# Adding the three shifted bit patterns of an exponential quad on GpSimd as 64-bit integers instead of on VectorE as 16-bit values

## The chip, the core and the metric

The kernel runs on one core of a Trainium2 chip. The metric is the device time of one execution in microseconds (us), taken as the median of several runs. A core has five engines with a queue of instructions each, which they work off in order and which wait for each other by semaphores: TensorE (PE in the profile, with its weight loads as PEld), ScalarE (ACT), VectorE (DVE), GpSimd (POOL) and SyncE (SP, which here issues the transfers).

## The reference

Two branches over the same input `x` (2048 x 512) are mixed by a gate: softmax attention with 32 heads of width 16, and a long convolution whose filter is a sum of complex exponentials.

```python
def _A_ref(x, wqkv, wo):                       # attention, H = 32, Dh = 16
    qkv = (x @ wqkv).reshape(B, S, 3, H, Dh) ...
    scores = jnp.einsum("bhqd,bhkd->bhqk", q, k) * Dh ** -0.5
    p = _softmax(scores, axis=-1)
    return jnp.einsum("bhqk,bhkd->bhqd", p, v) ... @ wo
def _B_ref(u, ...):                            # K = Re sum C dB exp(logdA * l); y = conv(u, K) + u * Dskip
    ...
g = _sigmoid((x * gate_w).sum(-1, keepdims=True))
return g * _A_ref(...) + (1 - g) * _B_ref(...)
```

The change lies in the exponential of the softmax. 32 heads x 2048 queries x 2048 keys are 134 million exponentials.

## The kernel before

**Tiles.** The scores are made in tiles of 128 keys x 512 queries of one head, 2048 tiles in all. Three tiles form a group; there are 683 groups, numbered `g`. A group's scores are written by `qk(g)` into one of two PSUM tensors of three banks, `SC[g % 2]`. `ex(g)` is one ScalarE activation (line 961 in the profile) over the group: it reads the scores from PSUM and writes bf16 exponentials to the ring `ET` (or `EX`, which is more of the same ring). `pv(q)` multiplies the exponentials of four heads (a quad) with the values and sums them in the PSUM bank `OA`; a column of ones among the values gives the softmax's denominator.

**Exponentials on VectorE.** For some quads the exponential is not made by ScalarE. In four groups that follow each other, the third tile of the group goes to VectorE instead, so that ScalarE's activation of such a group covers two tiles (128x1024) and not three (128x1536). VectorE's `bits(g)` (line 982) reads that tile from PSUM, multiplies and adds, and writes the result as a 16-bit integer into a quarter of the tile `DZ`: read as bf16 this bit pattern is a coarse power of two. When four quarters are there, `batch(i)` (line 996) makes three copies `DU` of all 2048 columns, each with another constant of `CUTS = (26, 56, 94)` added to the 16-bit pattern. `sums(i)` multiplies `DZ` and the three `DU` with the values, so that each such exponential is a sum of four coarse ones. Four tiles, their three adds and four products make a set `i`. Which groups give a tile is settled in `decide`, by the two windows in

```python
WIN = ((110,560,2,5,0,1),(560,678,4,5,0,2))
```

(first and last group, number of `DZ` tiles, least distance of two sets in groups, a budget that is 0 here, number of `DU` triples). A set is taken when its distance is kept, when no more than one set per 5.3 groups would have been taken, and by a planner's estimate of how far VectorE and ScalarE are: `idle()` is the later of the two engines' planned ends less VectorE's planned busy time, and `slow` in `win` widens the least distance to 9 groups while the convolution's filter blocks (`K0` to `K15`, built with VectorE) are behind a due line.

**Order.** All orders are planned in Python while the kernel is built. `Prog` keeps a planned end for every engine and instruction from written-out costs (`c=`) and delays (`lat=`); `Sched.fill` picks, group by group, the work of TensorE, VectorE, GpSimd and SyncE that is ready in the plan, by priority. The result is a fixed order per engine. TensorE's order between `qk(g+1)` and `qk(g+2)` is filled up to a planned amount; where real work lacks, products with the zero tile `wm` are put there.

**What depends on what around the adds.** An add of set `i` needs the four quarters of `DZ` (VectorE) and the products of the set that used the same `DU` before (TensorE): in the first window there is one triple of `DU`, in the second there are two. A product of `DU` needs its add. A new group's scores, `qk(g+2)`, need `ex(g)` to have read the same PSUM tensor and, for a third tile that VectorE takes, `bits(g)` too. GpSimd does a few fills and index patterns in the first 13 us and nothing after that.

Of the kernel before, what the change touches and what calls it, by code (L numbers as in the profile page):

```python
# [11 lines left out]
ALU = mybir.AluOpType  # L12
# [91 lines left out]
class Buf:  # L104
# [20 lines left out]

    def u16(self, off, dims):
        return self(off, dims).bitcast(U16)

    def b16(self, off, dims):
        t = self(off // 2, [[1, 1]]).bitcast(BF16)  # L130
        return bass.AP(tensor=t.tensor, offset=t.offset + off % 2, ap=[list(t.ap[0])] + [list(d) for d in dims])
# [5 lines left out]
class Prog:  # L137
# [113 lines left out]
    def op(self, eng, fn, R=(), W=(), c=.1, lat=.085, a=0, cfg=None):  # L251
        if self.cap is not None:
            self.cap.append((self.op, (eng, fn, R, W), dict(c=c, lat=lat, a=a, cfg=cfg)))
            return
        if cfg is not None:
            if cfg != self.cfg:
                c += TURN[cfg]
            self.cfg = cfg
        self.act += a
        self.log.append((self.op, self.q, (eng, fn, R, W)))  # L260
        deps = self._deps(eng, R, W)
        i = self.cnt[eng]
        at = self.tm[eng]
        for s, k in deps.items():
            at = max(at, self.fin[(s, k)] + (.03 if s == eng else .05))
        if eng == "PE" and len(self.pt) + 1 >= self.edge():
            at = max(at, self.land())
        self.tm[eng] = at + c
        if eng == "DVE":
            self.busy += c  # L270
        self.fin[(eng, i)] = at + c + lat
        self.cnt[eng] += 1
        w = self._record(eng, fn, deps, eng, i, R, W)
        if eng == "PE":
            b = self.edge()
            self.pt += [at] * (2 + max(w - 1, 0))
            if len(self.pt) > b:
                self.av.append(max(self.pt[b - LEAD] + F1, self.av[-1] + F2))
        return at + c + lat
# [406 lines left out]
def record(nc, p, B, ins):  # L686
# [5 lines left out]
    op, dma = p.op, p.dma  # L692
# [230 lines left out]
    def zbank():  # L923
        if sch.now is not None:
            return OA, [(OA, 0, sch.now)]
        if sch.lock.get("MB") is None:
            st = MB.st.get(0, [{}, {}])
            last = [p.fin[(s, i)] for d in st for s, i in d.items() if s != "PE"]
            if max(last, default=0.0) + ZLAG <= p.tm["PE"]:
                return MB, [(MB, 0, "zero")]  # L930
        return None
# [46 lines left out]
    def bits(g):  # L978
        i, k = vec[g]
        sc, z = SC[g % 2], sets[i]["z"]  # L980
        yield ("DVE", .6, -1)
        op("DVE", lambda v: v.tensor_scalar(z.u16(512 * k, [[1, 512]]), sc(1024, [[1, 512]]), XS, XB, ALU.mult, ALU.add),  # L982
           [(sc, 2, g)], [(z, k, (i, k))], c=.605)
        sch.mark(f"bits{g}")
        if k == 3:
            sch.add(batch(i), 0)

    def batch(i):
        z, us, q, b = (sets[i][x] for x in ("z", "u", "q", "b"))
        R = [(z, k, (i, k)) for k in range(4)]  # L990
        sch.add(sums(i), 0)
        if sets[i]["olu"] is not None:
            yield ("AFTER", f"dvp{sets[i]['olu']}")
        for n, (u, cut) in enumerate(zip(us, CUTS)):
            yield ("DVE", .6)
            op("DVE", lambda v, u=u, cut=cut: v.tensor_scalar(u.u16(0, [[1, 2048]]), z.u16(0, [[1, 2048]]), float(cut), None, ALU.add),  # L996
               R, [(u, 0, i)], c=.07 + 2048 / 3840)
            sch.mark(f"u{i}.{n}")

    def sums(i):  # L1000
        z, us, q, b = (sets[i][x] for x in ("z", "u", "q", "b"))
        yield ("AFTER", f"pv{16 * b}")
        if i:
            yield ("AFTER", f"dvp{i - 1}")
        for n, t in enumerate([z] + us):
            if n:
                yield ("AFTER", f"u{i}.{n - 1}")
            yield ("PE", QUAD)
            for k, j in enumerate(sets[i]["js"]):
                pv_mm(4 * q + j, t, 512 * k, [(t, 0, i)] if n else [(z, x, (i, x)) for x in range(4)], QUAD if k == 0 else 0)  # L1010
        sch.mark(f"dvp{i}")
        sch.do(lambda: whole(b))
# [680 lines left out]
    for q4 in range(4):  # L1693
# [6 lines left out]
        R, W = [(sc, sl, 'x0')], [(xT, (0, q4))]  # L1700
# [39 lines left out]
    for g in range(NG):  # L1740
# [8 lines left out]
        if g + 1 < NG:  # L1749
# [13 lines left out]
            if g + 1 in vec:  # L1763
                i = sets[vec[g + 1][0]]["old"]
# [12 lines left out]
        while lack >= 256 and p.tm["PE"] < t + OVER and g < NG - 1:  # L1777
            z = zbank()
# [79 lines left out]
```

## Time and profile before

| | |
|---|---|
| Time, median of 3 runs (lowest to highest) | 786.85 us (786.39 to 787.26) |
| Span of the profiled execution | 784.0 us |
| Difference of the median and the profiled span | 2.85 us |
| Groups (activations of scores) | 683, of them 373 of two tiles |
| Sets on VectorE | 93, that is 372 tiles and 279 adds |
| HBM read and written | 63.81 MB and 19.42 MB, 106 GB/s over the span |

The profile is of one execution. Its span is the time between the first and the last instruction; the runs' median is 2.85 us above it, and this difference is carried as it is in every sum. "Busy" counts an engine's instructions; a row of a group of instructions ends with its busy time, the mean of one in nanoseconds, and the idle time before its instructions with what ended it. Neighbouring instructions of one engine overlap at their ends, so the mean of one is more than the distance of two starts.

### The profile page before, as it was taken

The page shows a single profiled execution, that of the slowest core. Times are in us where ns is not written, and L with a number is a line of the kernel's source. Part 1 is how long each engine was busy: PE and PEld are TensorE (multiplying, and loading weights), DVE is VectorE, ACT ScalarE, POOL GpSimd, SP SyncE. Part 2 cuts the span into 40 slices and gives each one's busy share as a digit, 9 for nine tenths or more (in the row PEclk, how much of TensorE's full clock was granted, in tenths as well). Part 3 has the DMA queues.
Part 4 walks back from the last instruction along what each step waited for, and adds up shares of the span by engine and source line. Part 5 has one row for each costly group of instructions (what it writes and reads, how often), then busy time and mean ns, then how long its engine had stood idle before and what let it go on. Part 6 is the DMA issues. An engine that isn't in the chain of part 4 may idle for free.

```text
span 784.0 us, 31536 instructions
## 1 busy us (share of the span) xinstructions
PE 689.0 (88%) x14137; PEld 293.1 (37%) x14137; DVE 748.7 (96%) x1291; ACT 768.3 (98%) x694; POOL 11.3 (1%) x21
## 2 busy tenths in 40 slices
PE   7788778788778999989999989999889999989997
PEld 3233332222214544445444445444444444422222
DVE  7999999999999999999999999999999999999996
ACT  7999999999999999999999999999999999999996
POOL 5000000000000000000000000000000000000000
PEclk9999999999999999999999999999999999999999
DMA  9544212302002767685577835677746688831101
GB/s 208 90 102 89 63 40 92 116 31 59 5 9 51 174 149 195 170 213 123 144 181 182 205 94 145 175 165 200 181 117 146 143 198 215 202 81 32 32 22 35
DMA packets 168425, 95.52 MB, mean 122 GB/s; under 512 B 117729, under 2 KB 148834, under 8 KB 167906
## 3 DMA queue, kind: packets, MB, share of 16 engines
q1 hardware_dynamic: 166274, 92.33, 48.2%
q8 instruction: 111, 1.82, 1.1%
q10 hardware_dynamic: 2016, 1.18, 0.7%
q14 instruction: 24, 0.20, 0.1%
HBM read 63.81 MB, written 19.42 MB: 106 GB/s over the span
## 4 chain that ended last, share of the span: by engine, by line
ACT 93%; PE 2%; DMA 2%; DVE 0%; SPq 0%; issue 0%; ACTq 0%
ACT ET L961 84%; ACT EX L961 9%; DMA H<-gm_kd 2%; PE SC L701 1%; DMA Wk<-in_A_wqkv_dram 1%; PE MB L701 1%; PE OA L701 0%; SPq L1669 0%; ACTq L705 0%; DVE DZ L982 0%; SPq L1464 0%; ACT fo L1821 0%; DVE T L1040 0%; DVE KT L798 0%; DVE OT L1016 0%
## 5 line engine op out<-in xcount | busy, mean ns | idle before, releaser
L961 ACT ACTIVATE ET<-SC 128x1024 bf16<-128x1024 f32 (+1 forms) x612 | 696.6, 1472 | 2.2 <-PE SC L701 2.2
L701 PE MATMUL SC<-Qm,KT 32*128 32x512 bf16 x2048 | 273.1, 385 | 78.5 <-ACT ET L961 67.7
L982 DVE TENSOR_SCALAR DZ<-SC 128x512 uint16<-128x512 f32 x372 | 248.8, 684 | 13.0 <-PE SC L701 10.7
L996 DVE TENSOR_SCALAR DU<-DZ 128x2048 uint16<-128x2048 uint16 x279 | 182.8, 686 | 0.7
L701 PEld LDWEIGHTS SC<-Qm,KT 32*128 32x128 bf16 x2048 | 69.9, 91 | 274.2 <-ACT ET L961 217.3
L701 PE MATMUL OA<-ET,VE 128*32 128x512 bf16 x1516 | 158.0, 389 | 0.4 <-DVE OT L1016 0.2
L701 PE MATMUL OA<-wm 32*128 32x512 bf16 (+3 forms) x810 | 153.0, 342 | 1.2 <-DVE wm L754 1.2
L701 PE MATMUL OA<-DU,VE 128*32 128x512 bf16 x1116 | 104.8, 385 | 0.0
L701 PEld LDWEIGHTS MB<-U,H 128*32 128x32 bf16 x4096 | 82.8, 144 | 28.2 <-issue 15.0
L701 PE MATMUL MB<-U,H 128*32 128x128 bf16 (+7 forms) x4096 | 89.2, 224 | 2.3 <-DMA H<-gm_kd 2.2
L961 ACT ACTIVATE EX<-SC 128x1024 bf16<-128x1024 f32 (+1 forms) x71 | 82.6, 1403 | 1.0 <-PE SC L701 1.0
L701 PEld LDWEIGHTS OA<-ET,VE 128*32 128x32 bf16 x1516 | 40.8, 94 | 71.0 <-issue 67.1
L1040 DVE TENSOR_TENSOR T<-B,DT 128x1536 bf16<-128x1536 bf16 x64 | 58.9, 947 | 0.0
L701 PEld LDWEIGHTS MB<-T,Z 128*32 128x32 bf16 x2048 | 46.6, 152 | 11.3 <-issue 5.7
L701 PE MATMUL MB<-T,Z 128*32 128x64 bf16 (+1 forms) x2048 | 48.0, 235 | 0.0
L701 PEld LDWEIGHTS OA<-wm 128*32 128x32 bf16 (+2 forms) x810 | 40.2, 94 | 13.7 <-issue 11.2
L701 PEld LDWEIGHTS OA<-DU,VE 128*32 128x32 bf16 x1116 | 28.5, 96 | 36.6 <-issue 27.4
L701 PE MATMUL OA<-DZ,VE 128*32 128x512 bf16 x372 | 36.7, 383 | 0.0
L1016 DVE STREAM_TRANSPOSE OT<-OA 128x512 f32<-128x512 f32 x32 | 22.7, 709 | 2.9 <-PE OA L701 2.8
L1496 DVE TENSOR_TENSOR Yst<-MB,gt 128x512 bf16<-128x512 f32 x32 | 22.0, 686 | 2.2 <-PE MB L701 1.4
L701 PE MATMUL OA<-EX,VE 128*32 128x512 bf16 x160 | 23.0, 387 | 0.2 <-ACT ET L961 0.2
L1040 DVE TENSOR_TENSOR ft<-Z,DM 128x1024 bf16<-128x1024 bf16 x32 | 21.5, 681 | 0.0
(145 smaller groups left out, 439.8 us busy)
## 6 DMA issues: line engine op xcount, KB each, us to landing
H<-gm_kd SPq DMA_DIRECT2D x128, 256.0 KB, 4.2
U<-gm_xs SPq DMA_DIRECT2D x128, 134.2 KB, 3.8
T<-B SPq DMA_DIRECT2D x16, 256.0 KB, 4.2
gm_yd<-Yst SPq DMA_DIRECT2D x64, 64.0 KB, 3.3
gm_bd<-B16s SPq DMA_DIRECT2D x3, 1024.0 KB, 4.6
B<-gm_bd SPq DMA_DIRECT2D x12, 256.0 KB, 4.0
gm_kd<-Ks SPq DMA_DIRECT2D x64, 40.0 KB, 3.6
gm_xs<-xP SPq DMA_DIRECT2D x16, 136.0 KB, 3.9
```

The source lines that it names most:

```text
L701: op("PE", lambda t: t.matmul(out(), lhsT(), rhs(), start=start, stop=stop, skip_group_check=True, **kw), R, W, c=c, lat=.15, a=a, cfg=cfg)
L961: op("ACT", lambda a: a.activation(E(at, [[1, 512 * n]]), sc(0, [[1, 512 * n]]), AF.Exp, scale=DH ** -0.5), [(sc, i, g) for i in range(n)] ...
L982: op("DVE", lambda v: v.tensor_scalar(z.u16(512 * k, [[1, 512]]), sc(1024, [[1, 512]]), XS, XB, ALU.mult, ALU.add), [(sc, 2, g)], [(z, k, ...
L996: op("DVE", lambda v, u=u, cut=cut: v.tensor_scalar(u.u16(0, [[1, 2048]]), z.u16(0, [[1, 2048]]), float(cut), None, ALU.add), R, [(u, 0, i ...
L1016: op("DVE", lambda v: v.transpose(OT(512 * w, [[1, 512]]), OA(0, [[1, 512]])), [(OA, 0, b)], [(OT, w, b)], c=.64)
L1040: op(eng, lambda v: v.tensor_tensor(o(), a(), b_(), f), R, W, c=c)
L1496: op("DVE", lambda v, w=w, h=h: v.tensor_tensor(Yst(1024 * w + 4 * h, [[128, R8], [8, 16], [1, 4]]), MB(0, [[1, R8], [R8, 16], [NC, 4]]), ...
```

## The change

In `batch`, the three adds of a set move from VectorE's queue to GpSimd's. VectorE added a constant to 2048 values of 16 bits per partition. GpSimd adds a 64-bit constant, which holds the 16-bit constant four times, to 512 values of 64 bits per partition, on the same bytes. The tiles, their number and the products do not change. The planner is told 1.1 us for an add, in place of 0.6 us. Nothing else in the source changes, `WIN`, the rate of 5.3 and the due lines neither.

```diff
+    def u64(self):
+        return self(0, [[1, self.free]]).bitcast(mybir.dt.uint64)
+
...
         for n, (u, cut) in enumerate(zip(us, CUTS)):
-            yield ("DVE", .6)
-            op("DVE", lambda v, u=u, cut=cut: v.tensor_scalar(u.u16(0, [[1, 2048]]), z.u16(0, [[1, 2048]]), float(cut), None, ALU.add),
-               R, [(u, 0, i)], c=.07 + 2048 / 3840)
+            yield ("POOL", 1.1)
+            op("POOL", lambda v, u=u, cut=cut: v.int64_add(u.u64(), z.u64(), cut * 0x0001000100010001), R, [(u, 0, i)], c=1.1, lat=.1)
             sch.mark(f"u{i}.{n}")
```

Since the planner counts VectorE's planned work, the orders of all engines are planned anew, and more sets come out: 105 in place of 93 (420 tiles on VectorE in place of 372, and 315 adds in place of 279). Of ScalarE's 683 activations 421 cover two tiles, in place of 373. The products of `DU` go from 1116 to 1260 and those of `DZ` from 372 to 420; those of `ET` and `EX` go from 1676 to 1628, and the products with the zero tile in steps of 512 and 256 columns by 32 from 600 to 384.

GpSimd's queue ended with the fill of `gt`. Behind it there is now this (the engine's whole work from there on; each `ISA` row with a tile is one add; `DZ_56` and `DZ_57` are the two `DZ` tiles and `DU_58` to `DU_60` the one triple of the first window; the names in brackets are the semaphores waited for):

```order
L1545 MEMSET gt 128x128
L999 ISA
L999 ISA DU_58<-DZ_56 128x1024 [waits s_d6,s_d5,s_DVE,s_d4,s_d3]
L999 ISA DU_59<-DZ_56 128x1024
L999 ISA DU_60<-DZ_56 128x1024
L999 ISA DU_58<-DZ_57 128x1024 [waits s_POOL,s_PE,s_DVE]
L999 ISA DU_59<-DZ_57 128x1024
L999 ISA DU_60<-DZ_57 128x1024
```

The three adds of a set follow each other; the first waits for VectorE's last quarter and for TensorE's products of the set before. Lines are three higher than before, from the new helper.

VectorE's order in the first window, where sets are dense, was before:

```order
L982 TENSOR_SCALAR DZ_57<-SC 128x512
L996 TENSOR_SCALAR DU_58<-DZ_56 128x2048
L982 TENSOR_SCALAR DZ_57<-SC 128x512
L996 TENSOR_SCALAR DU_59<-DZ_56 128x2048
L982 TENSOR_SCALAR DZ_57<-SC 128x512 x2
L996 TENSOR_SCALAR DU_60<-DZ_56 128x2048
L1496 TENSOR_TENSOR Yst<-MB,gt 128x128x4
L982 TENSOR_SCALAR DZ_56<-SC 128x512
L996 TENSOR_SCALAR DU_58<-DZ_57 128x2048
```

and is now, in the same window (`T` and `ft` are tables of the filter, `Kt` a finished piece of it, `OT` the attention's sums):

```order
L1042 TENSOR_TENSOR T_150<-B_146,DT 128x1536
L985 TENSOR_SCALAR DZ_57<-SC 128x512 x2
L1042 TENSOR_TENSOR T_150<-B_146,DT 128x1536
L1404 STREAM_TRANSPOSE Kt<-MB 128x512
L985 TENSOR_SCALAR DZ_57<-SC 128x512
L1407 CAST Ks_154<-Kt 128x2x4x8x8
L1410 CAST Ks_154<-Kt 128x2x4x7
L1410 CAST Ks_154<-Kt 128x2x32
L985 TENSOR_SCALAR DZ_56<-SC 128x512 x4
```

The adds between the quarters are gone, and the filter's work and the next quarters stand there.

TensorE's order around the second and third add of a set is now (in the first window; `s_POOL` is what GpSimd signals):

```order
L704 MATMUL OA<-DU_59,VE 32x512 [waits s_POOL]
L704 MATMUL OA<-DU_59,VE 32x512 x3
L704 MATMUL SC<-Qm,KT 128x512 [waits s_ACT]
L704 MATMUL SC<-Qm,KT 128x512
L704 MATMUL SC<-Qm,KT 128x512 [waits s_DVE]
L704 MATMUL OA<-ET,VE 32x512 x4
L704 MATMUL OA<-DU_60,VE 32x512 [waits s_POOL]
L704 MATMUL OA<-DU_60,VE 32x512 x3
L704 MATMUL SC<-Qm,KT 128x512 [waits s_ACT]
```

The products of the adds stand ahead of the next groups' scores, about one add to a group, and wait for GpSimd where they waited for VectorE.

## The prediction

> **What bounds the kernel now.** I read the busy shares first, then the chain of work that ended last.
>
> ```profile
> PE 689.0 (88%) x14137; PEld 293.1 (37%) x14137; DVE 748.7 (96%) x1291; ACT 768.3 (98%) x694; POOL 11.3 (1%) x21
> ACT 93%; PE 2%; DMA 2%; DVE 0%; SPq 0%; issue 0%; ACTq 0%
> ACT ET L961 84%; ACT EX L961 9%; DMA H<-gm_kd 2%; PE SC L701 1%; DMA Wk<-in_A_wqkv_dram 1%; PE MB L701 1%; PE OA L701 0%; SPq L1669 0%; ACTq L705 0%; DVE DZ L982 0%; SPq L1464 0%; ACT fo L1821 0%; DVE T L1040 0%; DVE KT L798 0%; DVE OT L1016 0%
> ```
>
> ScalarE sets the end: its exponentials make 93% of the chain and it idles about 16 us of 784.0. VectorE, though 96% busy, is not on the chain. So VectorE's relief is worth nothing by itself. It counts only as far as it takes tiles from ScalarE, and whatever makes ScalarE wait costs its full length. The next view groups ScalarE's work by shape (busy time, mean of one).
>
> ```profile
> L961 ACT ACTIVATE ET<-SC 128x1536 bf16<-128x1536 f32 x292 | 422.4, 1716 | 2.2 <-PE SC L701 2.2
> L961 ACT ACTIVATE ET<-SC 128x1024 bf16<-128x1024 f32 x320 | 326.2, 1249 | 0.0
> L961 ACT ACTIVATE EX<-SC 128x1024 bf16<-128x1024 f32 x53 | 58.7, 1299 | 1.0 <-PE SC L701 1.0
> L961 ACT ACTIVATE EX<-SC 128x1536 bf16<-128x1536 f32 x18 | 29.5, 1708 | 0.0
> ```
>
> The mean of one holds the overlap with its neighbour. The pace is read from TensorE's scores, which wait for each activation, in the order of time (start, length):
>
> ```profile
> 142.20 0.39 PE L701 MATMUL SC<-Qm,KT 32*128 32x512 bf16 x3 [0.40 <-ACT ET L961]
> 143.54 0.39 PE L701 MATMUL SC<-Qm,KT 32*128 32x512 bf16 x1 [0.51 <-ACT ET L961]
> ...
> 402.70 0.39 PE L701 MATMUL SC<-Qm,KT 32*128 32x512 bf16 x1
> ...
> 403.62 0.39 PE L701 MATMUL SC<-Qm,KT 32*128 32x512 bf16 x3
> ```
>
> A group of three tiles takes 143.54 - 142.20 = 1.34 us, a group of two 403.62 - 402.70 = 0.92 us. A tile is worth 0.42 us to ScalarE.
>
> **Term 1, tiles taken from ScalarE.** The new plan has 105 sets in place of 93, so 48 activations shrink from three tiles to two. 48 x 0.42 = 20.2 us off ScalarE's queue. The means (1716 - 1249 = 467 ns) would give 22.4 us, the upper bound; I take 20.2. TensorE has for it 12 x 3 more steps of four products with `DU`. Eight of them take 0.62 us where four take 0.40, so a step adds about 0.22 us:
>
> ```profile
> 407.13 0.62 PE L701 MATMUL OA<-DU,VE 128*32 128x512 bf16 x8
> 408.46 0.40 PE L701 MATMUL OA<-DU,VE 128*32 128x512 bf16 x4
> ```
>
> 36 x 0.22 = 8 us. I cost them at nothing: 216 narrow products with the zero tile leave the order (54 steps of four, at half a step to a whole one 6 to 12 us). Without that cover it would be 8 us on an engine that is 88% busy.
>
> **Term 2, VectorE.** These groups matter, all from 140 us to the end (the last five read two tiles from SBUF each):
>
> ```profile
> L982 DVE TENSOR_SCALAR DZ<-SC 128x512 uint16<-128x512 f32 x372 | 248.8, 684 | 13.0 <-PE SC L701 10.7
> L996 DVE TENSOR_SCALAR DU<-DZ 128x2048 uint16<-128x2048 uint16 x279 | 182.8, 686 | 0.7
> L1040 DVE TENSOR_TENSOR T<-B,DT 128x1536 bf16<-128x1536 bf16 x64 | 58.9, 947 | 0.0
> L1040 DVE TENSOR_TENSOR ft<-Z,DM 128x1024 bf16<-128x1024 bf16 x32 | 21.5, 681 | 0.0
> L1040 DVE TENSOR_TENSOR Z<-ft,ft 128x1024 bf16<-128x1024 bf16 x24 | 16.4, 682 | 0.1
> L1040 DVE TENSOR_TENSOR ft<-Z,DL 128x1024 bf16<-128x1024 bf16 x16 | 10.8, 683 | 0.0
> L1031 DVE TENSOR_TENSOR ON<-OT,Rz 128x512 bf16<-128x512 f32 x13 | 8.9, 682 | 0.0
> ```
>
> The adds' 182.8 us go, 48 x 0.684 = 32.8 us of `bits` come: 748.7 - 182.8 + 32.8 = 598.7 us, some 78% of the shorter span. That is hidden under ScalarE, as before, and brings nothing of its own.
>
> **Term 3, the add on GpSimd.** No row has this operation, or any that reads SBUF on GpSimd. The nearest are fills and index patterns:
>
> ```profile
> L771 POOL MEMSET VE<- 128x2240 bf16 x4 | 7.7, 1965 | 0.3 <-DVE piota L759 0.3
> L725 POOL MEMSET Dr<- 128x512 bf16 x1 | 0.5, 525 | 0.3 <-POOLq L1843 0.3
> L751 POOL IOTA idf<- 128x128 f32 x1 | 0.2, 234 | 0.0
> L748 POOL IOTA piota<- 128x1 f32 x1 | 0.1, 133 | 0.0
> ```
>
> From 512 to 2240 elements a fill grows by (1965 - 525) / 1728 = 0.83 ns an element, with 0.1 us fixed. The index pattern, which computes and writes 32-bit values, grows by (234 - 133) / 127 = 0.80 ns. An add has 1024 words of 32 bits per partition to read and to write. Lower bound: reading and arithmetic hide behind the writes, 0.1 + 1024 x 0.83 ns = 0.95 us. Upper bound: read, add with carry and write follow each other, 0.1 + 3 x 0.85 = 2.65 us. Reading and writing apart would be 1.8 us. I take 1.1 us: the index pattern shows arithmetic at no cost per word, and 0.15 us is left for the reading to start. GpSimd is then busy 315 x 1.1 = 347 us in the 625 us from 145 to 770 us, 55%. In the densest stretch a set has five groups, 4 x 0.92 + 1.34 = 5.0 us, for its 3.3 us. The bare `ISA` row ahead of the first add falls into some 130 us in which GpSimd has nothing else to do.
>
> [...]
>
> What a longer add costs: its products stand right ahead of the next scores on TensorE, so scores, ScalarE and the rest queue behind the wait. The plan's orders count on 1.1 us, so the third add is late by 3 x (c - 1.1). TensorE's slack is in the waits (total, times, longest):
>
> ```profile
> PEld SC L701 <- ACT ET L961: 226.9, 418, 1.2
> PEld SC L701 <- ACT EX L961: 25.1, 52, 0.9
> PEld OA L701 <- DVE DU L996: 2.0, 9, 0.2
> ```
>
> TensorE is early for the scores by (226.9 + 25.1) / 683 = 0.37 us a group. The scores take 0.39 us and have one more activation, 0.92 us, until ScalarE needs them: 0.53 us more. So about 0.9 us a set are absorbed, and up to c = 1.4 us nothing is lost. From there each set loses 3 x (c - 1.1) - 0.9 us. At 1.1 us the term is nothing; the third row says that the adds were almost never waited for either.
>
> **Term 4, the two engines' reading.** Before, VectorE had SBUF to itself beside GpSimd; no row shows both reading. The five two-input groups above are 149 instructions and 116.5 us. Bounds: nothing, or each waits for an add in progress and the other way round. VectorE: 149 x 55% x half an add of 1.1 us = 45 us. GpSimd: 315 x 116.5/625 x half of 0.78 us = 23 us. That is 68 us of waiting, which reaches ScalarE only past the slack. I take a tenth, 7 us: `bits`, the bulk of VectorE's work, reads PSUM, and after 600 us the tables `T` are no longer built, as two stretches of the view by windows show for that tile alone:
>
> ```profile
> 520.00:600.00 80.00, 8.73 (x384) 8.57 (x384) 14.72 (x16) 1.00 0.71 168
> 600.00:680.00 80.00, 3.04 (x128) 3.04 (x128) 0.00 (x0) 1.00 0.75 180
> ```
>
> (VectorE's time on `T` is the third busy column.)
>
> **Sum.** 784.0 - 20.2 + 7 = 770.8 us of span; with the 2.85 us by which the median lies above the profiled span, 773.6 us. I say **773 us**.
>
> **Rival 1, a slow add.** If reading and writing do not overlap (1.8 us), each set loses 3 x 0.7 - 0.9 = 1.2 us, 126 us in 105 sets: 784.0 - 20.2 + 126 + 2.85 = 893 us. It beats the gain from 20.2 / 105 = 0.19 us a set on, that is from c = 1.46 us. At 1.65 us it is 845 us; at the upper bound of 2.65 us, 3.75 us a set, 1160 us. For it: a 64-bit add needs two words, a carry and two writes, more than any row does. Against it: the 0.80 ns of the index pattern.
>
> **Rival 2, the engines in each other's way.** The add is quick, but half of the 68 us of term 4 reaches ScalarE: a two-input instruction that waits for an add holds up the `bits` behind it, and the scores wait for `bits`. 784.0 - 20.2 + 34 + 2.85 = 801 us, slower than before; it decides from 20.2 of 68 us, 30%. For it: the order puts tables, `ft` and quarters in turn on VectorE. Against it: VectorE now has some 165 us of idle time. [...]
>
> **Rival 3, the gain is eaten and no more.** Terms 1 and 4 cancel, or the twelve more sets wait elsewhere: 787 us. That the adds should not give the same bits I leave out: no 16-bit pattern here carries into its neighbour.
>
> **How the numbers follow.** Forecast 44% (763 to 785 us), rival 1 27%, rival 2 23%, rival 3 6%. A measurement of this kernel tells about 0.2% (1.6 us) from no change. Faster gets the forecast's 44%; 5% for the same; slower 51% from the rivals together, though each is less likely than the forecast. The range starts at 763 us (the 22.4 us of the means and no loss, 764.4, less a little) and goes to 880 us: it holds forecast, rivals 2 and 3, and rival 1 up to an add of about 1.75 us, a third of its weight; some 82%.
>
> **What would show it.** Term 1: 421 activations of 128x1024 and ScalarE's busy time at about 748 us. Term 3: the mean of the adds' row on GpSimd at 1.0 to 1.3 us, and waits of PE for POOL in single microseconds; over 1.46 us or with tens of us of such waits, rival 1. Term 4: T at 947 ns and `ft` at 681 ns as before and few waits of SC for DZ; longer means, or idle time before them that POOL ends, and ScalarE waiting for scores by tens of us, rival 2. The forecast is wrong if ScalarE's share of the chain falls well under 90%.

## The result, and the profile after

The change makes the kernel slower: 838.56 us (median of 4 runs, 837.29 to 843.55) against 787.06 us for the kernel before on the same chip, a ratio of 1.066 (95% interval 1.063 to 1.070). The forecast was 773 us. The first view of the profile after is the page's busy time and chain, as before:

```profile
span 835.2 us, 31654 instructions
PE 726.4 (87%) x14071; PEld 304.9 (37%) x14071; DVE 687.3 (82%) x1060; ACT 759.4 (91%) x694; POOL 387.2 (46%) x336
ACT 44%; DVE 25%; PE 16%; issue 6%; POOL 6%; DMA 2%; SPq 0%; DVEq 0%; ACTq 0%; POOLq 0%
```

ScalarE's share of the chain fell from 93% to 44%, and VectorE, which was not on the chain at all, has 25% of it, though it is busy 82% of the span and not 96%. The engine that was relieved has become one that is waited for. The groups of instructions by shape say how (busy time, mean ns of one):

```profile
L999 POOL INT64_ADD DU<-DZ x315 | 375.7, 1208 | 409.2 <-DVE DZ L985 274.9 <-DVE B L1225 134.3
L985 DVE TENSOR_SCALAR DZ<-SC 128x512 uint16<-128x512 f32 x420 | 281.2, 682 | 106.5 <-PE SC L704 105.7
L1042 DVE TENSOR_TENSOR T<-B,DT 128x1536 bf16<-128x1536 bf16 x64 | 74.5, 1182 | 0.0
L1042 DVE TENSOR_TENSOR ft<-Z,DM 128x1024 bf16<-128x1024 bf16 x32 | 31.8, 1007 | 0.0
L1042 DVE TENSOR_TENSOR Z<-ft,ft 128x1024 bf16<-128x1024 bf16 x24 | 23.8, 990 | 0.0
L1033 DVE TENSOR_TENSOR ON<-OT,Rz 128x512 bf16<-128x512 f32 x15 | 17.6, 1173 | 1.0
L1042 DVE TENSOR_TENSOR ft<-Z,DL 128x1024 bf16<-128x1024 bf16 x16 | 14.9, 942 | 0.0
L1410 DVE CAST Ks<-Kt 128x56 bf16<-128x56 f32 x16 | 12.2, 764 | 0.0
```

`T` was 947 ns and is 1182, `ft` was 681 and is 1007, `Z` was 682 and is 990, `ON` was 682 and is 1173. These rows read two tiles from SBUF each, beside adds that read SBUF as well. `DZ`, which reads one tile and reads it from PSUM, is unchanged at 682 ns (684 before). The last row is of another kind, a short cast with one SBUF input (187 ns before). The adds themselves are as quick as forecast, 1.04 us in the median against 1.1: the view of the tile `DU` gives least, median and greatest length.

```profile
L999 POOL INT64_ADD DU<-DZ x315: 1030/1040/1932, 173.3 to 822.7; - x158
```

A stretch of the timeline of both engines shows one meeting (start, length):

```profile
218.17 4.28 POOL L999 INT64_ADD DU<-DZ  x3 [4.84 <-DVE DZ L985]
...
218.00 0.68 DVE L1042 TENSOR_TENSOR ft<-Z,DL 128x1024 bf16<-128x1024 bf16 x1
218.60 1.52 DVE L1042 TENSOR_TENSOR ft<-Z,DM 128x1024 bf16<-128x1024 bf16 x1
220.04 0.68 DVE L985 TENSOR_SCALAR DZ<-SC 128x512 uint16<-128x512 f32 x1
220.64 0.92 DVE L1042 TENSOR_TENSOR Z<-ft,ft 128x1024 bf16<-128x1024 bf16 x1
```

Three adds of 1.04 us take 4.28 us in place of 3.12. The `ft` that starts behind the first add takes 1.52 us in place of 0.68, and the `DZ` behind it, one of the quarters that the next scores wait for, starts 0.84 us later than it could. Who waited for whom, in all (total, times, longest):

```profile
ACT ET L964 <- PE SC L704: 48.7, 83, 1.8
PEld OA L704 <- POOL DU L999: 47.1, 99, 1.1
PEld SC L704 <- DVE DZ L985: 36.0, 63, 1.6
PE SC L704 <- DVE DZ L985: 17.8, 39, 1.3
PE OA L704 <- POOL DU L999: 17.3, 40, 0.9
POOL piota L751 <- issue: 10.8, 1, 10.8
```

Before, ScalarE waited 2.2 us for scores, and the row of the scores' weight loads for `DZ` was this:

```profile
PEld SC L701 <- DVE DZ L982: 2.7, 8, 0.5
```

Both `DZ` and the adds are waited for now; which of the two costs the time, this view does not tell. Its last row is a third thing: at the very start GpSimd stands still for 10.8 us ahead of its first index pattern, from which the identity for the first transposes is made. By stretches (busy time of PE, PEld, DVE, ACT, POOL; then the granted clock), the loss lies at the start and, above all, where VectorE builds tables:

```profile
0.00:40.00 40.00, 25.34 (x390) 10.68 (x390) 26.25 (x52) 25.77 (x23) 11.53 (x21) 1.00 0.59 119
...
200.00:280.00 80.00, 69.52 (x1168) 26.15 (x1164) 73.36 (x104) 70.86 (x65) 40.21 (x31) 0.89 0.29 75
280.00:360.00 80.00, 72.58 (x1486) 33.38 (x1488) 71.66 (x101) 69.93 (x67) 47.41 (x37) 0.94 0.52 132
360.00:440.00 80.00, 71.74 (x1576) 34.21 (x1574) 76.00 (x105) 69.77 (x67) 49.20 (x37) 0.98 0.52 131
...
600.00:680.00 80.00, 73.70 (x1589) 33.46 (x1585) 50.23 (x75) 79.20 (x78) 44.11 (x43) 1.00 0.82 181
```

ScalarE is idle 9 to 10 us of each 80 from 200 to 520 us, and 0.8 us from 600 to 680 us, where GpSimd adds about as busily; the tables `T` are built from 200 to 600 us and not after. The granted clock, the last column but two, is lower here than before (0.970 over the span in place of 0.998), but the idle time does not follow it: 9.1 us at 0.89, 10.2 us at 0.98.

### The profile page after: what moved, and what is told of

Its sections match the earlier page's. It is cut to its first block, busy times and chain, and to the rows that moved or that the text cites. A ratio compares the mean times of both kernels' runs of the same rounds, so it can differ in the third digit from the quotient of the medians.

```text
span 835.2 us, 31654 instructions
## 1 busy us (share of the span) xinstructions
PE 726.4 (87%) x14071; PEld 304.9 (37%) x14071; DVE 687.3 (82%) x1060; ACT 759.4 (91%) x694; POOL 387.2 (46%) x336
## 4 chain that ended last, share of the span: by engine, by line
ACT 44%; DVE 25%; PE 16%; issue 6%; POOL 6%; DMA 2%; SPq 0%; DVEq 0%; ACTq 0%; POOLq 0%
ACT ET L964 38%; DVE DZ L985 9%; PE SC L704 6%; ACT EX L964 6%; POOL DU L999 6%; PE OA L704 5%; PE MB L704 4%; DVE ft L1042 4%; DVE T L1042 3%; DVE Z L1042 2%; DMA H<-gm_kd 2%; DVE ON L1033 1%; DVE Kt L1404 1%; DVE OT L1018 1%; DVE Ks L1407 1%
## 5 line engine op out<-in xcount | busy, mean ns | idle before, releaser
L964 ACT ACTIVATE ET<-SC 128x1024 bf16<-128x1024 f32 (+1 forms) x615 | 687.9, 1311 | 50.6 <-PE SC L704 48.7
L999 POOL INT64_ADD DU<-DZ x315 | 375.7, 1208 | 409.2 <-DVE DZ L985 274.9
L985 DVE TENSOR_SCALAR DZ<-SC 128x512 uint16<-128x512 f32 x420 | 281.2, 682 | 106.5 <-PE SC L704 105.7
L704 PE MATMUL SC<-Qm,KT 32*128 32x512 bf16 x2048 | 300.6, 394 | 66.8 <-ACT ET L964 40.8
L704 PE MATMUL OA<-DU,VE 128*32 128x512 bf16 x1260 | 127.0, 394 | 18.6 <-POOL DU L999 17.3
L964 ACT ACTIVATE EX<-SC 128x1024 bf16<-128x1024 f32 (+1 forms) x68 | 75.2, 1253 | 0.6 <-PE SC L704 0.6
L1042 DVE TENSOR_TENSOR T<-B,DT 128x1536 bf16<-128x1536 bf16 x64 | 74.5, 1182 | 0.0
L704 PE MATMUL OA<-DZ,VE 128*32 128x512 bf16 x420 | 44.2, 408 | 0.0
L1042 DVE TENSOR_TENSOR ft<-Z,DM 128x1024 bf16<-128x1024 bf16 x32 | 31.8, 1007 | 0.0
L1042 DVE TENSOR_TENSOR Z<-ft,ft 128x1024 bf16<-128x1024 bf16 (+1 forms) x26 | 25.9, 994 | 0.0
```

The costliest lines, as they stand in the source:

```text
L704: op("PE", lambda t: t.matmul(out(), lhsT(), rhs(), start=start, stop=stop, skip_group_check=True, **kw), R, W, c=c, lat=.15, a=a, cfg=cfg)
L964: op("ACT", lambda a: a.activation(E(at, [[1, 512 * n]]), sc(0, [[1, 512 * n]]), AF.Exp, scale=DH ** -0.5), [(sc, i, g) for i in range(n)] ...
L999: op("POOL", lambda v, u=u, cut=cut: v.int64_add(u.u64(), z.u64(), cut * 0x0001000100010001), R, [(u, 0, i)], c=1.1, lat=.1)
L1042: op(eng, lambda v: v.tensor_tensor(o(), a(), b_(), f), R, W, c=c)
```

## The experiments

Theory: VectorE's two-input instructions and the adds hold each other up, and code for GpSimd is loaded anew at the start. Rivals: the new plan itself, any access by GpSimd, late adds on TensorE.

**Fills in place of the adds.** The order and the waits of every engine stay; GpSimd writes as many words and reads nothing.

```diff
-v.int64_add(u.u64(), z.u64(), cut * 0x0001000100010001)
+v.memset(u.f32(), 0.0)            # 1024 words of 32 bits
```

> The changed kernel with each 64-bit add replaced by a fill of the same 1024 words of DU with zero: the same orders and waits on every engine, GpSimd busy about as long (a fill of 1024 words by the rows of before about 0.95 us, the add's median is 1.04 us), but GpSimd reads nothing from SBUF and needs no second code library. It leaves out the three shifted patterns, so the output is not the reference's. Theory (two engines that read SBUF hold each other up, plus a late start): T back to 947 ns and ft to 681 ns, 765 to 772 us. Rival A (the new plan itself starves ScalarE, whatever GpSimd does): still over 800 us. Rival B (any GpSimd access to SBUF holds VectorE up, writing too): T and ft stay near 1180 and 1000 ns, over 800 us. Short casts SBUF to SBUF (Ks, 188 ns before, 764 ns after) tell the same for instructions with one SBUF input: back to 188 ns if only reading counts, still long if they are held by writes.

Measured: 774.31 us beside 786.20 us of before, a ratio of 0.984 (0.980 to 0.988). The groups of this run:

```profile
L999 POOL MEMSET DU<- 128x1024 f32 x315 | 292.6, 967 | 433.8 <-DVE DZ L985 433.8
L1042 DVE TENSOR_TENSOR T<-B,DT 128x1536 bf16<-128x1536 bf16 x64 | 59.3, 947 | 0.0
L1042 DVE TENSOR_TENSOR ft<-Z,DM 128x1024 bf16<-128x1024 bf16 x32 | 21.3, 677 | 0.0
L1410 DVE CAST Ks<-Kt 128x56 bf16<-128x56 f32 x16 | 10.5, 654 | 0.0
L1410 DVE CAST Ks<-Kt 128x64 bf16<-128x64 f32 x16 | 9.9, 621 | 0.0
```

`T` and `ft` are back at 947 and 677 ns beside a GpSimd that is nearly as busy (292.6 us of fills, 375.7 us of adds). So the adds, which read and write, hold two-input instructions up (1182 and 1007 ns), and the fills, which only write, do not; and the plan itself is good for a gain. Rival A falls. Rival B holds for one kind only: the short casts from SBUF to SBUF are longer beside the writes as well (654 and 621 ns). The first of them was before:

```profile
L1408 DVE CAST Ks<-Kt 128x56 bf16<-128x56 f32 x16 | 3.0, 187 | 0.0
```

Beside the adds this cast took 764 ns, but the 128x64 one behind it 183 ns; why the adds spare the second is not shown. The time is 2 us above the expected stretch.

**Code for GpSimd.** First the kernel before with one small add that nobody waits for:

```diff
+op("POOL", lambda g: g.int64_add(B["scr"].u64(), B["scr"].u64(), 1), [(B["scr"], 0)], [(B["scr"], 0)], c=.2)
```

> The kernel before with one 64-bit add of 16 values on a scratch tile after GpSimd's early fills, which nothing waits for. Theory (a program that holds index patterns and 64-bit adds loads GpSimd code anew at its start, and the index patterns that the first transposes need come late): the index pattern starts at 12.4 us in place of 1.7 us and the time is 8 to 10 us over before, 795 to 797 us. Rival (the 10.8 us ahead of the index pattern in the changed kernel is a chance of that run, or hidden by other late starts): 787 us, the same as before.

Measured: 794.27 us beside 786.20, a ratio of 1.011 (1.008 to 1.014), 0.7 us below the expected stretch and well clear of the rival's 787 us. Then the changed kernel with one index pattern behind its last add (the version with restored code, by the theory's name):

```diff
+op("POOL", lambda g: g.iota(pio(3, [[1, 1]]), [[0, 1]], base=0, channel_multiplier=1, ...), [], [(pio, 3)])
```

> The changed kernel with one index pattern more on GpSimd behind its last add, so that the code of the index patterns is in place again when an execution ends. Theory (the late start is the loading of code that the execution before has displaced): the index pattern starts at 1.7 us again and the time falls by 8 to 10 us, to 829 to 831 us. Rival (the code is loaded anew at every start of a program with both kinds): no change, 838 us.

Measured: 827.34 us, 11.2 us under the changed kernel. The first index pattern in the timelines of the changed kernel, of the kernel before with one add, and of this one:

```profile
12.40 0.14 POOL L751 IOTA piota<- 128x1 f32 x1 [10.80 <-issue]
```

```profile
11.91 0.14 POOL L752 IOTA piota<- 128x1 f32 x1 [10.30 <-issue]
```

```profile
1.89 0.13 POOL L751 IOTA piota<- 128x1 f32 x1 [0.29 <-issue]
```

Before, it started at 1.65 us, as it did with the fills. The wait is absent in the two programs without adds, 0.29 us with an index pattern behind the last add, and 10.30 and 10.80 us long in the programs with adds and no index pattern behind them. Two more waits of this sort show in the timelines, ahead of the one add in the kernel before and ahead of the last index pattern in the version with restored code:

```profile
27.71 0.58 POOL L1423 INT64_ADD scr<-scr  x1 [6.08 <-issue]
```

```profile
821.53 0.14 POOL L1793 IOTA piota<- 128x1 f32 x1 [7.21 <-issue]
```

The second ends 4 us before the span does (825.6 us). The waits come and go as the theory says; what GpSimd does in them, the loading of code by the theory, no view shows. The gain of 11.2 us was a little more than expected.

**Half adds.** Two adds of 256 values in place of one of 512.

```diff
+for h in range(2):
+    op("POOL", lambda v, ..., h=h: v.int64_add(u.u64(h), z.u64(h), cut * 0x0001000100010001), R, [(u, h, i)], c=.55, lat=.1)
```

> The changed kernel with each add cut into two of 256 values (half the columns), so that one instruction is about half as long and the sum on GpSimd about 0.1 us longer per add. Theory (a VectorE instruction with two SBUF inputs waits for the end of the add in progress, and an add for the end of that instruction): VectorE's waits about halve (T towards 1060 ns, ft towards 840 ns, short Ks casts towards 450 ns), and the time falls by 10 to 25 us, to 814 to 828 us. Rival (the engines share the reading at a finer grain than an instruction): T and ft unchanged, 838 us or a little more from the longer adds.

Measured: 840.6 us, no gain where 10 to 25 us were expected. The expectation missed in the long instructions too:

```profile
L1000 POOL INT64_ADD DU<-DZ x630 | 443.6, 723 | 346.3 <-DVE DZ L985 212.8 <-DVE B L1226 133.5
L1043 DVE TENSOR_TENSOR T<-B,DT 128x1536 bf16<-128x1536 bf16 x64 | 70.9, 1121 | 0.0
L1043 DVE TENSOR_TENSOR ft<-Z,DM 128x1024 bf16<-128x1024 bf16 x32 | 30.5, 967 | 0.0
L1411 DVE CAST Ks<-Kt 128x56 bf16<-128x56 f32 x16 | 7.9, 496 | 0.0
```

`T` went from 1182 to 1121 ns only, `ft` from 1007 to 967. The short cast waits about half as long, as expected. A half has a median of 612 ns, so that two cost 0.18 us more than one add, and its mean is 111 ns above that: 630 x 0.111 = 70 us of waiting on GpSimd in place of 53. TensorE's waits for adds rise from 64 to 126 us. That long instructions and halves take turns would fit, but was only argued. The granted clock was 0.991 here against 0.97 in the changed kernel, at about the same time; since the waits for adds have grown meanwhile, this alone does not tell what the lower clock costs.

**Products that do not wait for adds.** The last two candidates, on the version with restored code: TensorE multiplies `DZ` four times and never waits for GpSimd; the adds run as before. The order of every engine is the same.

```diff
-pv_mm(4 * q + j, t, 512 * k, [(t, 0, i)] if n else ...)
+pv_mm(4 * q + j, z, 512 * k, [(t, 0, i)] if n else ...)   # planned with DU, recorded as a reader of DZ alone
```

> e3_restore with the same order of instructions on every engine, but TensorE's products of the three shifted patterns read DZ itself in place of DU, so that TensorE never waits for GpSimd; the adds still run and still read DZ beside VectorE. The three shifts are left out of the result. It parts the 53 us between e3_restore (827.3 us) and e1_fills (774.3 us). Theory A (VectorE, held up by adds, is late with bits, and the scores wait for it): most of the 53 us stay, 808 to 825 us. Theory B (adds, held up by VectorE, are late for TensorE): most of them go, 776 to 792 us. In both T and ft stay at about 1180 and 1000 ns.

Measured: 822.65 us. Of the 53 us between 827.34 and 774.31 only 4.7 go (the kernel before took 786.87 us beside this run and 786.20 us beside the other two). Chain and waits of this run:

```profile
ACT 50%; DVE 31%; PE 13%; issue 5%; DMA 1%; SPq 1%; POOL 0%; DVEq 0%; ACTq 0%
...
PEld SC L709 <- DVE DZ L991: 48.8, 74, 1.9
ACT ET L970 <- PE SC L709: 46.7, 69, 1.7
DVE DZ L991 <- POOL DU L1005: 13.0, 12, 1.6
```

Theory A: the 48 us come by way of VectorE. An add holds up a table's instruction (`T` 1183 ns here, 947 before), the quarter behind it is late, the scores wait for the quarter, ScalarE for the scores. The last row is new in this run: twelve quarters wait for an add that still reads their tile. What part of the 48 us is that is not shown.

**Longer fills.** Each fill in four pieces.

```diff
+[v.memset(u.f32(h), 0.0) for h in range(4)][-1]           # 256 words each
```

> e1_fills with each fill cut into four of 256 words, so that GpSimd is busy about 1.2 us for what was 0.97 us, which is the mean of an add in the changed kernel with its waiting in it; it still reads nothing from SBUF. The three patterns are left out of the result. Prediction's slack (an add of up to 1.4 us costs nothing): 772 to 780 us. Rival (the mean length of an add by itself makes TensorE late): 790 us or more.

Measured: 770.37 us, a ratio of 0.980 (0.976 to 0.984). The pieces overlap and are busy 332.3 / 315 = 1.05 us an add, not 1.2, so the slack up to 1.4 us was not tried. The run shows that 1.05 us of GpSimd's time in place of an add costs nothing by itself, and the short `Ks` casts wait less (342 and 294 ns) beside shorter writes.

**Adds on GpSimd only in the second window**, where no tables are built, with the sets of before:

```diff
+if sets[i]["w"] < 1: ... VectorE's add as before
+else: ... GpSimd's add
```

> The kernel before with its 93 sets in the same groups; only the 69 adds of the second window, where VectorE builds no more tables, run on GpSimd, and an index pattern at the end restores the code. Theory (an add costs only beside two-input work on VectorE): the same as before, 785 to 789 us, adds at 1.04 to 1.08 us. Rival (each add costs 53/315 = 0.17 us wherever it stands): 798 us.

Measured: 788.74 us beside 786.87, a ratio of 1.003 (1.001 to 1.005): the 69 adds cost about 2 us (0.8 to 3.5), with a mean of 1061 ns, and not the 12 us of the rival. In this window they do little harm. The window differs from the first in a second way, four `DZ` tiles and two `DU` triples in place of two and one, and this run does not part the two. Few tiles alone cost little: with the fills ScalarE was idle 0.3 to 1.2 us of each 80 from 200 to 520 us, on the same tiles.

**A version meant to beat both.**

```diff
+WIN = ((110,430,2,5,0,1),(430,672,4,4,0,2)); SL = 12; KB = 19.0; RATE2 = 4.5; XR = 430
```

> A version meant to beat both: the filter is built earlier (due lines 19 groups apart in place of 26.8, sets 12 groups apart while it is behind), with its 39 sets added on VectorE as before; from group 430 on, 57 sets, 4 groups apart, are added on GpSimd; code restored at the end. 96 sets in place of 93 take 3 x 4 x 0.42 = 5 us from ScalarE. Theory: 778 to 784 us. Rival (the convolution's products and their loads, now squeezed to the end, or the denser sets on TensorE, take the place): 787 us or more.

Measured: 785.1 us beside 786.87, a ratio of 0.999 (0.997 to 1.001). This is 1.1 us above the expected stretch, and no difference from before that can be told.

**Honest prices in the plan.** The planner is told the lengths measured beside adds (`T` +0.24 us, `ft` and `Z` +0.32, `ON` and `Rz` +0.5, one `Ks` cast +0.58), first alone, then with sets moved to the end.

```diff
-H10 = dv(1024, 2)
+H10 = dv(1024, 2) + 0.32
```

> e3_restore with the planner told what VectorE's instructions took beside the adds: T 0.24 us more, ft, Z 0.32, ON and Rz 0.5, one short Ks cast 0.58. The plan then has 102 sets in place of 105 and leaves VectorE room around its tables. Theory (the loss is quarters that stand too close behind instructions that come out longer than planned): a good part of the 48 us that e5_no_wait left goes, 785 to 800 us. Rival (which instruction meets an add is chance, and mean prices do not help): 815 us or more.

> e7_priced with the sets moved towards the end: due lines of the filter 22 groups apart, second window from group 450 with sets 4 groups apart (52 sets in each window, 104 in all). Fewer adds stand beside the tables. Theory: 5 to 10 us under e7_priced, 776 to 792 us, so it may beat the kernel before. Rival (the end is then set by the convolution, as in late_dense): no better than e7_priced.

Measured: 804.96 and 803.68 us beside 785.66 (ratios 1.026 and 1.023). The version with restored code was 41 us above before; the first of these is 19 us above it, with all adds still on GpSimd beside the tables (102 sets in place of 105, and new orders). The waits of the first of the two:

```profile
ACT ET L964 <- PE SC L704: 16.8, 40, 1.6
PEld SC L704 <- DVE DZ L985: 18.6, 34, 2.1
```

ScalarE waits 16.8 us for scores in place of 49.5, though `T` is as long as ever (1187 ns). Both times are above what was expected. One part of the rest stands at the very end: the single wait of ScalarE between its last exponentials and the last output, in the kernel before and in the two priced versions.

```profile
ACT fo L1821 <- PE SC L701: 4.1, 1, 4.1
ACT fo L1825 <- PE SC L704: 15.5, 1, 15.5
ACT fo L1831 <- PE SC L705: 25.9, 1, 25.9
```

TensorE is there still multiplying the output's projection and the convolution's finished rows, 11 and 22 us longer than before. This is the rival of the second run: work squeezed to the end sets the end. No version that computes the reference's output beats the kernel before.

## Why the prediction was wrong

- **Term 1 (48 tiles, 20.2 us).** The tiles left ScalarE as counted: 369 + 52 activations of two tiles. What reached the end without the adds was 786.20 - 774.31 = 11.9 us with whole fills and 786.87 - 770.37 = 16.5 us with fills in pieces. The mechanism was right: in the profile of the whole fills ScalarE is busy 748.0 us in place of 768.3, 20.3 us less. Its span is 16.0 us shorter; of the 4.3 us between, 2.7 are the wait at the very end (6.8 us in place of 4.1) and 1.6 waits for scores (3.8 in place of 2.2). Why the median gains less than this profile is not shown.
- **Term 2 (VectorE's relief is hidden).** Wrong in its consequence. VectorE was busy 687 us in place of the 599 worked out. Beside the fills, on the same plan, it was busy 628 us, some 20 us of it the two short casts of 654 and 621 ns. Of the 59 us from there to 687, the rows of its instructions grow by 46 us beside the adds; where the rest comes from is not shown. Being idle 18% of the time did not help, because what counts is when a quarter is done, not how much VectorE does.
- **Term 3 (the add).** Right: 1.04 us against 1.1 taken, 1.0 ns a word beside the index pattern's 0.80 ns, and rival 1 falls. TensorE's waits for adds cost 4.7 us. But one sentence of it failed, the bare `ISA` row "falls into some 130 us in which GpSimd has nothing else to do". Ahead of the first add that holds: GpSimd idles 134.3 us there, put down to VectorE. The price came at the start of an execution: 10.8 us of waiting ahead of the first index pattern, and 11.2 us of time that an index pattern behind the last add takes off. That code was no longer in place there is the author's explanation; no view shows it.
- **Term 4 (the engines' reading).** This is the step that decided it. The waiting was sized well on VectorE: the five groups' means grew by 64 x 0.235 + 32 x 0.326 + 24 x 0.308 + 16 x 0.259 + 15 x 0.491 = 44 us, against 45 worked out; casts and small instructions, which were left out, add some 24. That only instructions with two SBUF inputs would wait was the author's assumption, which no row of before showed; beside the adds the cast with one SBUF input grew too (187 to 764 ns). On GpSimd it was 315 x 0.168 = 53 us against 23. What failed is "I take a tenth, 7 us": 827.34 - 774.31 = 53 us reached the time (that GpSimd's own waiting is 53 us too is chance), 48 of them through VectorE. The reason given, that `bits` reads PSUM, was true of `bits` (682 ns beside the adds, 684 before) and beside the point: `bits` stands behind a two-input instruction in the same queue (0.84 us late behind the `ft` of 1.52 us). The 0.9 us of slack was worked out for late adds on TensorE. Its first part, 0.37 us by which TensorE is early for the scores, does not count for a quarter that the scores themselves wait for, and single waits for a quarter were up to 1.6 us long; how much of the slack was left for them is not shown.
- **The rivals.** Rival 2 had the place and the mechanism, at 801 us. With the 53 us measured in place of its 34, and 11.2 us of start that no case had, it comes to 784.0 - 20.2 + 53 + 11.2 + 2.85 = 831 us, and with the 4 to 8 us that term 1 fell short to 835 to 839 us. That this meets the measured 838.56 us proves nothing by itself, since the 53, the 11.2 and the shortfall are differences of the same runs.

Open stay how VectorE and GpSimd choose who goes first when both wait, what part the lower clock (0.89 in one stretch of the changed kernel) has, why it is lower, and what makes up the rest of the some 19 us that the priced plans lose, beside the longer end.

## What to carry to other kernels

In this kernel work moved to GpSimd had two prices: its own length (1.04 us an add), and what it did to the instructions of VectorE that read two tiles from SBUF (`T` 947 to 1182 ns) or copy from SBUF to SBUF (a short cast 187 to 764 ns), and then to whatever stood behind those in VectorE's queue. Ask which of VectorE's results is waited for soonest; where it stood behind such an instruction, idle time on VectorE (18% of the span) was no cover. Adds on GpSimd behind index patterns were paid for at the start of an execution (10.8 us of waiting); an index pattern put at the end took 11.2 us off the time.

## What the runs showed of the hardware

- A 64-bit add of 512 values by 128 partitions on GpSimd took 1.04 us in the median, 1.0 ns a 32-bit word, against a mean of 0.967 us for a fill of as many words.
- GpSimd stood still 10.1 to 10.8 us ahead of its first index pattern in the programs with adds and no index pattern behind them, 6.7 to 7.5 us ahead of an index pattern put behind the last add, and 6.08 us ahead of the one add in the kernel before, with no instruction in the profile beside it.
- Beside GpSimd's adds, which read and write SBUF, two-input instructions on VectorE were longer, and beside its fills, which only write, they were not (`T` 1182 and 947 ns); beside the fills short casts from SBUF to SBUF were longer (187 to 654 ns and 190 to 621 ns).
